# Linear attention, a gated mixer and a gated convolution: every engine's order from a list schedule, and the last weights split early through HBM

## The chip, the cores and the metric

The kernel runs on one core of a Trainium2 chip. The metric is the device time of one execution in microseconds.

## The reference, cut to what matters

All tensors are fp32, with B = 8 batches, H = 8 heads, S = 576 tokens, D = 64, d_model = 512 and d_ff = 1024. Three stages follow each other:

```python
# 1 attention: softmax of q over D, of k over S
kv = einsum('bhsd,bhse->bhde', softmax_s(k), v)
x  = einsum('bhsd,bhde->bhse', softmax_d(q), kv)      # to [B, S, 512]
# 2 gated mixer
h = gelu(x @ w_in); u, v = halves(h)
v_n = (v - mean) / sqrt(var + 1e-6) * g_ln
x = x + (u * (w_sg @ v_n + b_sg)) @ w_out
# 3 gated convolution over tokens
h = relu(x @ w_in2)                                   # [B, S, 1024]
out = (h * sigmoid(conv3(h, conv_w))) @ w_out2
```

## The kernel before, in words

Every large product is made of three single-pass matmuls (`mm3`, lines 62 to 65): each operand is split into a high part and a low part, and hi·hi, hi·lo and lo·hi are summed in PSUM. So each operand needs two vector steps: ScalarE copies the high part (a rounding copy), and VectorE or GpSimd subtracts it to get the low part. The weights arrive in a 64-bit format and are taken apart by `Split` (lines 70 to 151): a job loads a slice (line 92), and then ScalarE (lines 99, 102, 109), VectorE (lines 100, 101, 107, 110) and GpSimd (lines 111, 119, 120) make its high and low parts. There are 12 jobs of 512 columns for stage two's weights, one for the convolution's, and 32 jobs of 256 columns for stage three's: 16 for `w_in2` and 16 for `w_out2`, with four VectorE operations each, on the tiles `s` and `t`.

For each batch, stages one and two run these groups on TensorE: `back_kv` (line 349, 40 small products for k times v; `kvd` is the normalised result), `xt` and `xt_left` (lines 389 and 376: x from q and `kvd`, evacuated into `xh` and `xl`), `hv` (line 408, four token tiles and in five batches a fifth one, `hv_pair`, each of 12 matmuls of 512 columns), `hu` (line 458, 8 groups of 12 of 288 columns), `mx` (line 468, 8 groups of 14 of 288) and `wo` (line 489, 8 groups of 12 of 288). After an `hv` come gelu on ScalarE, the statistics and the normalisation on VectorE (`bn_stats`, lines 418 to 422), a power on GpSimd (line 421), and the split of the result into `vnh` and `vnl`. After an `mx` come `u` (line 479), `gh` and `gl` (lines 483 and 484). `x` before and after the mixer goes to HBM (`xld`, `x2d`). The softmaxes of the next batches' k and q are cut into steps (`k_steps`, `q_steps`, lines 215 and 274). Batch 0 has a softmax of its own, on other layouts (`s_k` to `s_qtl`, lines 560 to 608).

Stage three runs after all batches of stage two: `h2` (line 818, 16 groups of 12 matmuls of 288 columns for each batch), the convolution and the sigmoid (lines 830 to 841), and `o2` (line 857, 8 groups of 12 of 512 columns, with 24 more for each two batches for the left-over tokens).

What sets the order: a string (`CFG['start']`, line 32) gives the start, and `PLAN` says after which of the 29 groups of a batch a step of k, of q or of a weight split is put in. GpSimd keeps the order in which the code was written. The other engines' instructions are ordered by the framework's scheduler, which can also interleave the matmuls of different groups. The 32 jobs of stage three's weights run from batch 6's eighth group to the middle of stage three's first batch (`w2["in"].step()` and `w2["out"].step()`), since their buffers take the place of the attention's tiles.

Of the kernel before, what the change touches and what calls it, by code (L numbers as in the profile page):

```python
# [1 line left out]

# [19 lines left out]
PLAN = {  # L22
# [6 lines left out]
}  # L29
PLAN = {s: {i: [(c, 1) for c in t] for i, t in p.items()} for s, p in PLAN.items()}  # L30
# [4 lines left out]

@with_exitstack
def attn_gated_conv_kernel(ctx, tc, q, k, v, q0, k0, w_in, g_ln, w_sgT, b_sg, w_out, w_in2, conv_w, w_out2, out):
    nc = tc.nc
    dve, act, pool, pe, sp = nc.vector, nc.scalar, nc.gpsimd, nc.tensor, nc.sync
# [3 lines left out]
    ctx.enter_context(tc.manual_schedule(engines={mybir.EngineType.Pool}))  # L43
    dram = ctx.enter_context(tc.tile_pool(name="dram", bufs=1, space=bass.MemoryType.DRAM))
    ps_mm = ctx.enter_context(tc.tile_pool(name="ps_mm", bufs=4, space=bass.MemoryType.PSUM))
    ps_acc = ctx.enter_context(tc.tile_pool(name="ps_acc", bufs=1, space=bass.MemoryType.PSUM))
    keep = ctx.enter_context(tc.tile_pool(name="keep", bufs=1))
    xp = ctx.enter_context(tc.tile_pool(name="xp", bufs=1))

    x2d = [dram.tile([128, KC, S], F32, name=f"x2d{b}") for b in range(B)]  # L50
    xld = [dram.tile([128, KC, S], F32, name=f"xld{b}") for b in range(B)]

    def mm_tile():
        return ps_mm.tile([128, 512], F32, tag="mm", name="mm")
# [15 lines left out]
    class Split:  # L70
        def __init__(self, slots, jobs, mode):
            self.slots, self.jobs, self.mode = slots, jobs, mode
            self.loaded = self.done = 0

        def views(self, i):
            src, hi, lo, n = self.jobs[i]
            raw, a = self.slots[i % len(self.slots)]
            raw = raw[:, 0:2 * n].bitcast(U32)
            a = a[:, 0:n]
            if len(src.shape) == 4:  # L80
                g = src.shape[1]
                raw = raw.rearrange("p (g f two) -> p g f two", g=g, two=2)
                a = a.rearrange("p (g f) -> p g f", g=g)
                return src, raw, raw[:, :, :, 1], raw[:, :, :, 0], a, hi, lo
            raw = raw.rearrange("p (f two) -> p f two", two=2)
            return src, raw, raw[:, :, 1], raw[:, :, 0], a, hi, lo

        def load(self):
            i = self.loaded
            if i < len(self.jobs) and i < max(0, self.done - 1) + len(self.slots):  # L90
                src, raw = self.views(i)[0:2]
                sp.dma_start(raw, src)
                self.loaded += 1

        def p1(self, i):
            while self.loaded <= i:
                self.load()
            src, raw, h, l, a, hi, lo = self.views(i)
            act.activation(l.bitcast(F32), l, AF.Copy, scale=2.0 ** -52)
            dve.tensor_scalar(a.bitcast(U32), h, 3, 0x3FFFFFF8, ALU.logical_shift_left, ALU.bitwise_and)  # L100
            dve.scalar_tensor_tensor(a.bitcast(U32), h, 0xC0000000, a.bitcast(U32), ALU.bitwise_and, ALU.bitwise_or)  # L101
            act.activation(h.bitcast(F32), h.bitcast(F32), AF.Square)

        def p2(self, i):
            src, raw, h, l, a, hi, lo = self.views(i)
            lf, hf = l.bitcast(F32), h.bitcast(F32)
            dve.scalar_tensor_tensor(a, hf, GUARD * GUARD, a, ALU.is_ge, ALU.mult)
            if hi is not None:
                act.activation(hi, a, AF.Copy)  # L109
            dve.tensor_scalar(h, a.bitcast(U32), 0xFF800000, None, ALU.bitwise_and)  # L110
            (pool if hi is not None else dve).tensor_tensor(lf, lf, hf, ALU.mult)

        def p3(self, i):
            src, raw, h, l, a, hi, lo = self.views(i)
            if hi is None:
                dve.tensor_tensor(lo, a, l.bitcast(F32), ALU.add)
                return
            e1, e2 = self.mode(i)
            e1.tensor_tensor(a, a, r32(hi), ALU.subtract)
            e2.tensor_tensor(lo, a, l.bitcast(F32), ALU.add)  # L120

        def step(self):
            i = self.done
            if i > len(self.jobs):
                return
            if i > 0:
                self.p2(i - 1)
            if i < len(self.jobs):
                self.p1(i)
            if i > 0:  # L130
                self.p3(i - 1)
            self.done += 1
            self.load()

        def need(self, i):
            while self.done < i + 2:
                self.step()
# [22 lines left out]
    p1 = es1.enter_context(tc.tile_pool(name="p1", bufs=1, reuse_waits="tile"))  # L160
    wk = es1.enter_context(tc.tile_pool(name="wk", bufs=2, reuse_waits="tile"))
# [17 lines left out]
    at = es2.enter_context(tc.tile_pool(name="at", bufs=1, side="right", reuse_waits="tile"))  # L179
# [4 lines left out]
    scr = at.tile([128, 1024], F32, name="scr")  # L184
# [132 lines left out]
    class Stream:  # L317
# [657 lines left out]
```

## Time and profile before

| | |
|---|---|
| median of 3 runs | 1004.29 us (1003.51 to 1005.01) |
| the profiled execution | 1007.08 us, with a span of 1005.3 us |
| TensorE busy | 931.5 us (93%), 6080 matmuls |
| VectorE, ScalarE, GpSimd busy | 753.6, 450.8, 399.2 us |
| mean granted TensorE clock | 0.974 |
| DMA | 90.61 MB, 90 GB/s on average |

Busy time is the time in which an instruction of the engine was under way. Matmuls overlap in their pipeline, so what one costs is the distance from its start to the next one's start, not its duration. An engine works through its instructions in their order: one that waits holds up all behind it.

### The profile page before, as it was taken

The page shows a single profiled execution, that of the slowest core. Times are in us where ns is not written, and L with a number is a line of the kernel's source. Part 1 is how long each engine was busy: PE and PEld are TensorE (multiplying, and loading weights), DVE is VectorE, ACT ScalarE, POOL GpSimd, SP SyncE. Part 2 cuts the span into 40 slices and gives each one's busy share as a digit, 9 for nine tenths or more (in the row PEclk, how much of TensorE's full clock was granted, in tenths as well). Part 3 has the DMA queues.
Part 4 walks back from the last instruction along what each step waited for, and adds up shares of the span by engine and source line. Part 5 has one row for each costly group of instructions (what it writes and reads, how often), then busy time and mean ns, then how long its engine had stood idle before and what let it go on. Part 6 is the DMA issues. An engine that isn't in the chain of part 4 may idle for free.

```text
span 1005.3 us, 15903 instructions
## 1 busy us (share of the span) xinstructions
PE 931.5 (93%) x6080; PEld 835.1 (83%) x6080; DVE 753.6 (75%) x1354; ACT 450.8 (45%) x897; POOL 399.2 (40%) x469
## 2 busy tenths in 40 slices
PE   4665998989999999999989998899999999999998
PEld 3454977978989999898978987698999899989996
DVE  7999796867775676754888499787687758775863
ACT  6543635355536263361645355344344434443442
POOL 6447536437233071441575166632222322232210
PEclk9777998999999999999999999999999999999999
DMA  9721160451244212310332251213030303030001
GB/s 286 237 75 54 54 184 27 140 170 32 83 134 154 73 33 87 113 71 25 121 119 77 71 202 32 75 63 136 11 124 13 137 11 121 16 137 11 25 19 52
DMA packets 36580, 90.61 MB, mean 90 GB/s; under 512 B 3732, under 2 KB 14996, under 8 KB 32920
## 3 DMA queue, kind: packets, MB, share of 16 engines
q1 hardware_dynamic: 36504, 89.60, 27.4%
q8 instruction: 47, 0.77, 0.3%
q14 instruction: 29, 0.24, 0.1%
HBM read 62.46 MB, written 27.13 MB: 89 GB/s over the span
## 4 chain that ended last, share of the span: by engine, by line
PE 55%; DVE 22%; POOL 7%; issue 7%; ACT 6%; DMA 3%; SPq 0%; POOLq 0%; ACTq 0%; DVEq 0%
PE mm L63 10%; PE mm L65 10%; PE mm L64 10%; PE acc L63 7%; PE acc L64 7%; PE acc L65 7%; POOL kt L240 2%; POOL q L290 1%; DVE t L101 1%; PE mm L358 1%; DVE qm L285 1%; DVE t L100 1%; POOL rd L421 1%; DVE vnl L431 1%; DVE st L418 1%
## 5 line engine op out<-in xcount | busy, mean ns | idle before, releaser
L64 PE MATMUL mm<-xl,w2h 128*128 128x288 f32 x512 | 150.2, 295 | 0.6 <-DVE xl L813 0.6
L65 PE MATMUL mm<-xh,w2l 128*128 128x288 f32 x512 | 150.0, 295 | 0.0
L63 PE MATMUL mm<-xh,w2h 128*128 128x288 f32 x512 | 148.0, 295 | 1.9 <-ACT xh L812 1.9
L421 POOL TENSOR_TENSOR rd<-rd,nhalf 128x1 f32<-128x1 f32 x37 | 36.2, 982 | 176.2 <-DVE rd L420 171.0
L65 PE MATMUL acc<-wAh,yl 128*128 128x512 f32 x256 | 98.6, 393 | 4.7 <-DVE yl L841 4.7
L63 PE MATMUL acc<-wAh,yh 128*128 128x512 f32 x256 | 100.6, 393 | 1.6 <-ACT yh L840 1.6
L64 PE MATMUL acc<-wAl,yh 128*128 128x512 f32 x256 | 100.8, 394 | 0.0
L63 PEld LDWEIGHTS mm<-xh,w2h 128*128 128x128 f32 x512 | 95.2, 188 | 6.0 <-ACT xh L812 3.2
L64 PEld LDWEIGHTS mm<-xl,w2h 128*128 128x128 f32 x512 | 95.9, 188 | 3.8 <-DVE xl L813 1.4
L65 PEld LDWEIGHTS mm<-xh,w2l 128*128 128x128 f32 x512 | 96.0, 188 | 0.4
L65 PE MATMUL mm<-sgh,vnl 128*128 128x288 f32 x256 | 79.0, 309 | 8.2 <-DVE vnl L431 8.2
L65 PE MATMUL mm<-xh,wAl 128*128 128x288 f32 x256 | 77.2, 302 | 9.9 <-POOL wAl L120 6.3
L63 PE MATMUL mm<-sgh,vnh 128*128 128x288 f32 x256 | 81.7, 319 | 4.0 <-ACT v L414 2.2
L831 DVE SCALAR_TENSOR_TENSOR cv<-h,cw,cv 128x576 f32<-128x576 f32 x64 | 81.4, 1272 | 1.8
L63 PE MATMUL mm<-xh,wAh 128*128 128x288 f32 x256 | 79.4, 310 | 2.8 <-ACT wAh L109 2.7
L841 DVE TENSOR_TENSOR yl<-cv,yh 128x576 fp32r<-128x576 f32 x64 | 51.5, 804 | 37.5 <-ACT yh L840 37.4
L64 PE MATMUL mm<-sgl,vnh 128*128 128x288 f32 x256 | 78.3, 306 | 0.0
L64 PE MATMUL acc<-gl,wouth 128*128 128x288 f32 x256 | 74.1, 302 | 3.7 <-DVE gl L484 3.5
L838 ACT ACTIVATE cv<-cv 128x576 f32<-128x576 f32 x64 | 43.8, 686 | 74.5 <-DVE cv L832 73.9
L64 PE MATMUL mm<-xl,wAh 128*128 128x288 f32 x256 | 76.8, 300 | 0.0
L828 ACT ACTIVATE h<-mm 128x288 f32<-128x288 f32 x128 | 51.0, 407 | 54.6 <-PE mm L65 54.5
L844 POOL CAST yL1h<-yh 128x64 fp32r<-128x64 f32 x32 | 19.5, 611 | 139.3 <-ACT yh L840 139.3
(232 smaller groups left out, 2648.5 us busy)
## 6 DMA issues: line engine op xcount, KB each, us to landing
vt<-in_v SPq DMA_DIRECT2D x8, 1152.0 KB, 10.9
x2d<-x2s SPq DMA_DIRECT2D x16, 576.0 KB, 3.5
out<-ot SPq DMA_DIRECT2D x32, 256.0 KB, 2.0
kt<-in_k SPq DMA_DIRECT2D x7, 1152.0 KB, 5.3
xld<-xl SPq DMA_DIRECT2D x7, 1152.0 KB, 4.2
xf<-x2d SPq DMA_DIRECT2D x7, 1152.0 KB, 6.3
xg<-xld SPq DMA_DIRECT2D x7, 1152.0 KB, 5.1
q<-in_q SPq DMA_DIRECT2D x28, 256.0 KB, 2.9
```

Of the source, the lines that this page charges most:

```text
L63: pe.matmul(ps, ah, bh, start=start, stop=False)
L64: pe.matmul(ps, ah, bl, start=False, stop=False)
L65: pe.matmul(ps, al, bh, start=False, stop=stop)
L100: dve.tensor_scalar(a.bitcast(U32), h, 3, 0x3FFFFFF8, ALU.logical_shift_left, ALU.bitwise_and)
L101: dve.scalar_tensor_tensor(a.bitcast(U32), h, 0xC0000000, a.bitcast(U32), ALU.bitwise_and, ALU.bitwise_or)
L240: pool.tensor_tensor(kc, kc, bc, ALU.subtract)
L421: pool.tensor_tensor(rd, rd, nhalf, ALU.pow)
L828: act.activation(h[:, 1 + hf * HALF:1 + hf * HALF + HALF], ps, AF.Relu)
L831: dve.scalar_tensor_tensor(cv, h[:, 0:S], cw[:, fc:fc + 1], cv, ALU.mult, ALU.add)
L838: act.activation(cv, cv, AF.Sigmoid)
L841: dve.tensor_tensor(yl, cv, r32(yh), ALU.subtract)
L844: pool.tensor_copy(yL_hi[:, fc, o:o + 64], r32(yh[:, 512:576]))
```

## The change

Nothing that is computed changes, and the matmuls are the same. Three things change.

First, the kernel no longer issues instructions as its code runs. `Plan` records every instruction of all five engines, with the tile regions that it reads and writes (`View`, `Buf`, `Pool`), prices it with a formula per engine and operation (`price`), gives it a latest time that counts back from TensorE's groups in the order in which they were written (`deadlines`), and then runs a list schedule (`order`): at each moment a free engine takes the ready instruction with the earliest latest time. TensorE takes whole groups, the first of the next eight that would stall for at most 0.15 (the first) or 0.05. What comes out is issued in that order, and the framework orders nothing (`manual_schedule(engines=None)`). A formula for VectorE beside GpSimd lengthens both.

Second, `PLAN`, `Stream` and the string for the start are gone: `insert` says after which groups the attention of the next batch (`xt`, `back_kv`) and the softmax steps of the one after it (`attend_k`, `attend_q`) are recorded, and the schedule places them.

Third, the 32 split jobs are recorded at the start of batch 1 (`split_far`), work on two small slots (`wsl`, `farh`), and store their two halves to HBM (`w2d`, `wo2d`). After batch 6's attention is done, `open_w2` loads both halves back into SBUF, 8 loads of 128x4x256; `open_wo2` loads 16 of 128x512 late in batch 7. That adds 64 stores of 128x256 and 24 loads to SP's queue. The scratch tile of the k maxima is halved (`scr`), so `top` takes three maxima of 512 columns in place of one of 1024 and one of 512, and `h_t` of stage three moves to the pool of `w2`.

The core of the diff:

```diff
-    ctx.enter_context(tc.manual_schedule(engines={mybir.EngineType.Pool}))
+    plan = Plan({"pe": nc.tensor, "act": nc.scalar, "dve": nc.vector, "pool": nc.gpsimd, "sp": nc.sync})
+    dve, act, pool, pe, sp = plan.dve, plan.act, plan.pool, plan.pe, plan.sp
+    ctx.enter_context(tc.manual_schedule(engines=None))
...
-PLAN = {
-    0: {0: 'w', 1: 'ws', 2: 'sw', 3: 'ssw', 5: 'k', 8: 'wsw', 9: 'c', 11: 'qk', 12: 'ck', 14: 'w', 15: 'q', 16: 'kw', 18: 'kq', 19: 'kkq', 20: 'q', 21: 'q', 22: 'kqk', 23: 'qkqq', 25: 'qq', 27: 'kq', 28: 'qqw', 29: 'qqq'},
...
+    def deadlines(self):
+        t = 0.0
+        for n in self.nodes:
+            n.late = big
+            if n.eng == "pe":
+                n.late = t
+                t += n.cost
...
+        for n in reversed(self.nodes):
+            for s in n.succ:
+                c = n.lat if s.deps[n.i] == "end" else 0.0
+                n.late = min(n.late, s.late - c)
...
+            if n.eng == "dve" and n.shared and poolend[0] > t:
+                more = min(cost, poolend[0] - t) * 0.8
+                cost, lat = cost + more, lat + more
...
+    def split_far(src, d, k, n, behind):
+        for c in range(k):
+            for f in range(0, n, NW):
+                fs = slice(f, f + NW)
+                slot, h = parts[njob[0] % 2]
+                njob[0] += 1
+                split(slot, src[:, c, fs], far_h, slot[1].bitcast(F32R), NW, (pool, pool), [t[:, c, fs] for t in d], behind)
...
     def open_w2():
-        es2.close()
+        g = plan.gate(at.bufs, es2.close)
...
+            for n, d in zip(("hi", "lo"), w2d):
+                sp.dma_start(r32(w2[n][:, :, fs]), d[:, :, fs])
...
-            if (b == 6 and i >= 7) or (b == 7 and i < 24):
-                w2["in"].step()
-            if b == 7 and i >= 24:
-                w2["out"].step()
-                w2["out"].step()
+            if b == 1 and i == 0:
+                mark = next(n for n in reversed(plan.nodes) if n.eng == "pe")
+                split_far(w_in2_v, w2d, KC, FF2, mark)
+                split_far(w_out2_v, wo2d, NFC, DM, mark)
             g()
-            attend(b, i + 1)
+            insert(b, i)
```

How the instructions move, at the three places that the prediction speaks of, on VectorE and, at the third, on SP too. In the changed kernel all instructions are issued from one line, 394.

At the start, where batch 0's k times v is normalised into `kvd` (`rs` is the reciprocal of the sums; `wAl` and `sa` belong to a weight split, `qm` and `lm` to batch 1's softmax). Before:

```order
L365 TENSOR_SCALAR rs_278<-mm 128x2
L120 TENSOR_TENSOR wAl<-sb,sa 128x512
L107 SCALAR_TENSOR_TENSOR sa<-sa 128x24
L285 TENSOR_REDUCE qm<-q_351 128x16
L366 RECIPROCAL rs_278<-rs_278 128x2
L252 TENSOR_REDUCE lm<-q_255 128x8
L110 TENSOR_SCALAR sa<-sa 128x24
L285 TENSOR_REDUCE qm<-q_353 128x16
L369 TENSOR_TENSOR kvd<-mm,rs_278 64x2x64 x2
```

With the change:

```order
L394 TENSOR_TENSOR xl_0_122<-xl_0_122,wAh_238 128x512
L394 TENSOR_REDUCE sm_115<-sgh_91 128x4
L394 TENSOR_TENSOR sgh_91<-sgh_91,sm_115 128x256
L394 TENSOR_SCALAR rs_0_274<-mm_175 128x2
L394 RECIPROCAL rs_0_274<-rs_0_274 128x2
L394 TENSOR_TENSOR kvd_89<-mm_175,rs_0_274 64x2x64 x2
L394 TENSOR_REDUCE sm_115<-sgh_91 128x4
L394 TENSOR_SCALAR sm_115<-sm_115 128x4
```

The first `kvd` was VectorE's 51st row, with weight work and batch 1's softmax between its steps; now it is the 27th, with its steps together.

Near the end of batch 0, where batch 1's x is split into `xl` (the tile with number 1168 before, 948 now; `kt` and `scr` are the maxima of batch 2's k, `gl` the gate of batch 0). Before:

```order
L221 TENSOR_TENSOR scr<-scr 128x512
L384 TENSOR_TENSOR xLl<-mm,xLh 128x4x64
L395 TENSOR_TENSOR xl_1168<-mm,xh_1167 128x512
L484 TENSOR_TENSOR gl<-u,gh 128x288
L213 COPY qx<-qm 32x64 x4
L222 TENSOR_TENSOR scr<-scr,kt 64x256
L395 TENSOR_TENSOR xl_1168<-mm,xh_1167 128x512
L223 TENSOR_TENSOR scr<-scr,kt 64x256
```

With the change:

```order
L394 TENSOR_TENSOR scr_130<-scr_130,kt_149 64x256
L394 STREAM_TRANSPOSE scr_130<-scr_130 128x512
L394 TENSOR_TENSOR lt_0_324<-lt_0_324,wouth_745 128x512
L394 TENSOR_REDUCE r_0_494<-scr_130 128x16
L394 COPY r_0_519<-r_0_494 64x16 x2
L394 TENSOR_TENSOR r_0_494<-r_0_494,r_0_519 128x16
L394 COPY r_0_519<-r_0_494 32x16 x4
L394 TENSOR_TENSOR r_0_494<-r_0_494,r_0_519 128x16
L394 STREAM_TRANSPOSE scr_130<-r_0_494 128x512
L394 TENSOR_TENSOR xl_0_948<-mm_133,xh_0_902 128x512
```

Batch 1's `xl` stood behind nearly all of batch 0's gates, with batch 2's maxima between its parts. Now batch 2's maxima stand whole ahead of it, and half of batch 0's gates behind it: five of the eight `gl` have a later row.

The split of stage three's weights. Before, in batch 6, tiles `s` and `t`:

```order
L395 TENSOR_TENSOR xl_4883<-mm,xh_4882 128x512
L419 BN_AGGR mv<-st 128x2
L100 TENSOR_SCALAR t_4971<-s_4970 128x256
L420 TENSOR_SCALAR rd<-mv 128x1
L422 SCALAR_TENSOR_TENSOR v<-v,mv,g_bc 128x512
L101 SCALAR_TENSOR_TENSOR t_4971<-s_4970,t_4971 128x256
L100 TENSOR_SCALAR t_4973<-s_4972 128x256
L100 TENSOR_SCALAR t_4975<-s_4974 128x256
```

With the change, in batch 1, tile `wsl`:

```order
L394 TENSOR_SCALAR wsl_1266<-wsl_1266 128x256
L394 SCALAR_TENSOR_TENSOR wsl_1266<-wsl_1266 128x256
L394 TENSOR_TENSOR gl_848<-u_635,gh_826 128x288
L394 TENSOR_TENSOR xl_0_320<-mm_133,xh_0_306 128x512
L394 TENSOR_TENSOR xl_0_320<-mm_175,xh_0_306 128x512
L394 TENSOR_TENSOR u_681<-mm_187,u_681 128x288
L394 TENSOR_TENSOR gl_791<-u_681,gh_722 128x288
L394 TENSOR_TENSOR qm_373<-qm_373,qx_389 128x64
L394 TENSOR_TENSOR lm_369<-lm_369,lx_375 128x8
L394 SCALAR_TENSOR_TENSOR wsl_1266<-wsl_1266 128x256
```

The 128 VectorE operations of these jobs stood from batch 6 to stage three; now 12 stand in batch 1, 20, 20, 22, 30 and 24 in batches 2 to 6, one or two at a time, and none later. On SP the stores stand among the loads of the next batches, with the change (`q` is batch 5's, `x2d` takes batch 1's x after the mixer):

```order
L394 DMA w2dl_1683<-wsl_1266 128x256
L394 DMA x2d_0_1710<-x2s_124 512x1x288
L394 DMA w2dh_1611<-farh_1605 128x256
L394 DMA kt_149<-in_k 128x2304
L394 DMA vt_85<-in_v 128x36x64
L394 DMA wsl_1266<-in_w_in 128x512
L394 DMA w2dl_1683<-wsl_1266 128x256
L394 DMA q_1_135<-in_q 128x256
```

A store of a `farh` half stands right ahead of batch 4's k and v.

## Rows read from the trace of the kernel before

**Rows 1.** Busy time by stretch: length, PE, PEld, DVE, ACT, POOL, PE clock, DMA share, GB/s.

```profile
0.00:40.30 40.30, 18.79 (x132) 12.21 (x133) 34.66 (x73) 26.10 (x56) 22.97 (x32) 0.87 0.83 265
40.30:135.80 95.50, 73.37 (x456) 63.97 (x456) 86.16 (x145) 43.43 (x79) 54.88 (x46) 0.86 0.35 101
135.80:213.60 77.80, 71.27 (x542) 64.06 (x541) 58.65 (x144) 34.66 (x66) 38.76 (x39) 0.93 0.31 99
213.60:280.20 66.60, 64.35 (x469) 58.24 (x468) 50.56 (x115) 34.47 (x70) 26.12 (x26) 1.00 0.31 97
280.20:339.30 59.10, 59.10 (x446) 53.98 (x444) 38.92 (x97) 27.07 (x53) 16.66 (x17) 1.00 0.44 129
339.30:403.60 64.30, 63.42 (x465) 57.71 (x464) 45.19 (x97) 29.18 (x63) 26.23 (x26) 1.00 0.20 68
403.60:465.20 61.60, 60.76 (x449) 55.02 (x448) 37.39 (x86) 25.93 (x48) 20.70 (x21) 1.00 0.21 66
465.20:524.20 59.00, 57.07 (x358) 51.04 (x356) 46.45 (x100) 29.93 (x70) 33.49 (x42) 1.00 0.32 106
524.20:581.40 57.20, 53.44 (x353) 50.53 (x352) 37.54 (x85) 24.50 (x57) 22.53 (x29) 0.97 0.27 81
581.40:650.00 68.60, 59.24 (x352) 50.98 (x352) 62.54 (x103) 32.66 (x72) 46.83 (x56) 1.00 0.26 89
650.00:1005.30 355.30, 350.70 (x2075) 317.41 (x2073) 255.52 (x319) 142.87 (x267) 90.04 (x136) 1.00 0.18 65
```

**Rows 2.** Longest PE waits, whole span: us in total, times, longest.

```profile
PE mm L393 <- DVE kvd L369: 8.8, 1, 8.8
PE mm L65 <- DVE vnl L431: 8.2, 1, 8.2
```

**Rows 3.** Busy time, 75 to 100 us, columns as in Rows 1.

```profile
75.00:100.00 25.00, 12.96 (x60) 11.72 (x60) 22.98 (x20) 8.55 (x16) 19.49 (x16) 0.70 0.18 54
```

**Rows 4.** Timeline of DVE and then POOL near 84 us: start, duration, instruction.

```profile
83.88 8.97 DVE L670 TENSOR_TENSOR rhs<-sgs 2x576 fp32r<-2x576 f32 x1
...
87.32 4.91 POOL L240 TENSOR_TENSOR kt<-kt,scr 128x512 f32<-128x512 f32 x4
```

**Rows 5.** Timeline of PE: start us, duration, instruction; spacing of matmuls.

```profile
21.01 0.69 PE L358 MATMUL mm<-vt,kt 128*64 128x65 f32 x16
21.89 0.69 PE L358 MATMUL mm<-vt,kt 128*64 128x65 f32 x16
...
46.94 0.40 PE L63 MATMUL mm<-wAh,xh 128*128 128x512 f32 x1
51.63 0.39 PE L65 MATMUL mm<-wAh,xl 128*128 128x512 f32 x1
51.86 0.29 PE L63 MATMUL mm<-xh,wAh 128*128 128x288 f32 x1
53.56 0.29 PE L65 MATMUL mm<-xh,wAl 128*128 128x288 f32 x1
...
298.06 1.02 PE L393 MATMUL mm<-q,kvd 128*128 128x512 f32 x2
298.51 0.70 PE L63 MATMUL mm<-xh,wAh 128*128 128x288 f32 x1
...
1000.30 0.40 PE L65 MATMUL mm<-wAh,yL1l 128*128 128x512 f32 x1
```

**Rows 6.** Busy time on tile t, by stretch: length, DVE, ACT, POOL; the rest as Rows 1.

```profile
465.20:524.20 59.00, 23.70 (x50) 4.89 (x12) 19.33 (x24) 1.00 0.32 106
524.20:581.40 57.20, 16.39 (x35) 3.52 (x9) 13.44 (x17) 0.97 0.27 81
581.40:650.00 68.60, 22.47 (x45) 4.51 (x11) 22.93 (x24) 1.00 0.26 89
```

**Rows 7.** Line 100 on tile t: duration ns min/median/max, first and last start.

```profile
L100 DVE TENSOR_SCALAR t<-s x32: 262/316/873, 485.8 to 625.2; 128x256 uint32<-128x256 uint32 x32
```

**Rows 8.** Groups of ACT: one group of table loads.

```profile
L465 ACT ACT_TABLE_LOAD x9 | 11.5, 1283 | 1.6 <-DVE gl L484 1.4
```

More of the change, by code (lines that the diff above doesn't have):

```diff
@@ L68, in u64 @@
         return ap.bitcast(U32)
[L70 to L84, printed above, removed]
-            raw = raw.rearrange("p (f two) -> p f two", two=2)
[L86 to L137, printed above, removed]
@@ new lines, in split @@
+    def split(slot, src, hi, lo, n, modes, stores=(), behind=None):
+        raw, a = slot
+        raw = raw[:, 0:2 * n].bitcast(U32)
+        a = a[:, 0:n]
+        if len(src.shape) == 4:
+            g = src.shape[1]
+            raw = raw.rearrange("p (g f two) -> p g f two", g=g, two=2)
+            a = a.rearrange("p (g f) -> p g f", g=g)
+            h, l = raw[:, :, :, 1], raw[:, :, :, 0]
+        else:
+            raw = raw.rearrange("p (f two) -> p f two", two=2)
+            h, l = raw[:, :, 1], raw[:, :, 0]
+        lf, hf = l.bitcast(F32), h.bitcast(F32)
+        ld = sp.dma_start(raw, src)
+        if behind is not None:
+            ld.deps[behind.i] = "start"
+        act.activation(lf, l, AF.Copy, scale=2.0 ** -52)
+        dve.tensor_scalar(a.bitcast(U32), h, 3, 0x3FFFFFF8, ALU.logical_shift_left, ALU.bitwise_and)
+        dve.scalar_tensor_tensor(a.bitcast(U32), h, 0xC0000000, a.bitcast(U32), ALU.bitwise_and, ALU.bitwise_or)
+        act.activation(hf, hf, AF.Square)
+        dve.scalar_tensor_tensor(a, hf, GUARD * GUARD, a, ALU.is_ge, ALU.mult)
+        if hi is not None:
+            act.activation(hi, a, AF.Copy)
+        dve.tensor_scalar(h, a.bitcast(U32), 0xFF800000, None, ALU.bitwise_and)
+        (pool if hi is not None else dve).tensor_tensor(lf, lf, hf, ALU.mult)
+        if hi is None:
+            dve.tensor_tensor(lo, a, lf, ALU.add)
+            return
+        modes[0].tensor_tensor(a, a, r32(hi), ALU.subtract)
+        modes[1].tensor_tensor(lo, a, lf, ALU.add)
+        for t, d in zip((hi, lo), stores):
+            sp.dma_start(d, r32(t))
@@ L389, in xt @@
     def xt(b, hp):
+        plan.begin()
         if hp == 0:
@@ L408, in hv @@
     def hv(lh, ll, dst):
-        w1.need(3)
+        plan.begin()
         ps = mm_tile()
@@ L637, in s_sg @@
         sg_load(1)
[L639 to L651 removed]
+    for hp in range(4):
+        s_k(hp)
+    for t in range(5):
+        s_qa(t)
+    for hp in range(4):
+        s_kt(hp)
+    s_ktl()
+    for t in range(5):
+        s_qb(t)
+    for hp in range(4):
+        s_qt(hp)
+    s_qtl()
+    load_q(1)
+    load_left(1)
+    s_xl()
+    for c in range(2):
+        back_kv(0, c)
+    for hp in range(4):
+        xt(0, hp)
+    xt_left(0)
+    xt_copy(0)
+    for i, jb in enumerate(jobs):
+        split(slots[i % 3], *jb, MODES[i])
+        if i == 7:
+            split(csl[0], conv_v, None, cw, 3 * NFC, None)
+    s_sg()
     def sg_split(c):
@@ L759, in do_mx, with attend_k, attend_q, insert @@
         mx(b, j)
-    cj = Split(csl, [(conv_v, None, cw, 3 * NFC)], None)
-    cj.load()
+    def attend_k(b):
+        for f in k_steps(b):
+            f()
+    def attend_q(b):
+        for f in q_steps(b):
+            f()
+    def insert(b, i):
+        if b + 1 < B:
+            if b == 0 and i == 4:
+                attend_k(1)
+                attend_q(1)
+            if b == 0 and i in (8, 9):
+                back_kv(1, i - 8)
+            if b == 0 and i == 10:
+                xt_left(1)
+            if i in ((12, 14, 16, 18) if b % 2 == 0 else (8, 10, 12, 14)):
+                xt(b + 1, (i - (12 if b % 2 == 0 else 8)) // 2)
+            if b + 2 < B:
+                if i == 19:
+                    attend_k(b + 2)
+                    attend_q(b + 2)
+                if i in (23, 24):
+                    back_kv(b + 2, i - 23)
+                if i == 25:
+                    xt_left(b + 2)
+        if b == 6 and i == 20:
+            open_w2()
+        if b == 7 and i == 24:
+            open_wo2()
+        if b == 7 and i in (20, 21, 22, 23, 24):
+            x2_early(i - 20)()
     for b in range(B):
         if b == 1:
-            lt1[1] = p1.tile([128, DM], F32R, tag="lt11", name="lt11")
+            lt1[1] = p1.tile([128, DM], F32R, tag="lt11")
         groups = [lambda t=t: do_hv(b, t) for t in range(4)]
         groups += [lambda j=j: do_hu(b, j) for j in range(2)]
-        groups.insert(CFG['hvl'][min(b, 2)], lambda: do_pair(b))
+        groups.append(lambda: do_pair(b))
         for j in range(8):
```

553 lines of the change are left out of this document (401 added, 152 removed), and 5 rows, old and new, of the table PLAN.

## The prediction

> **What bounds the kernel now.** I read the busy time by stretch first, cut at the first `hv` matmul of each batch and at stage three's first `h2` (581.4 us) [rows 1]. The reader is to see three regimes. Until 135.8 us VectorE is the fullest engine (34.66 of 40.3 us, 86.16 of 95.5) while TensorE works 73.37 of 95.5, at a granted clock of 0.86, a mix of its two levels. Batches 2 to 7 (213.6 to 581.4) keep TensorE at 93 to 100%, with VectorE at 61 to 79%. From 581.4 to 650 VectorE is up to 62.54 of 68.6 and TensorE idles; after 650 TensorE is the bound. Then the longest waits of TensorE [rows 2]: 8.8 us for the first `kvd`, 8.2 us for a `vnl`, both on VectorE. In the stretch around the second, TensorE was busy 12.96 of 25 us and VectorE 22.98 [rows 3]. There one VectorE subtraction took 8.97 us, while GpSimd ran four subtractions of `kt` of 4.91 us [rows 4].
>
> **What TensorE must do.** The spacing of matmuls [rows 5] gives: 20 steps of 512 columns in 4.69 us, 0.2345 each; 13 steps of 288 in 1.70 us, 0.131 each; ten `kv` products in 0.88 us, 3.5 for 40; an `xt` pair 0.46, four of them 1.84; 0.8 for the left-over x is my estimate from that. A batch has 48 x 0.2345 = 11.3, 304 x 0.131 = 39.8, and 3.5 + 1.8 + 0.8: 57.2 us, or 60.0 with an `hv_pair` (2.8). Batches 2 to 7 need 60.0, 57.2, 60.0, 57.2, 55.7 (no `kv` left) and 51.1 (no attention left): 341.2. Stage three needs 1536 x 0.131 + 864 x 0.2345 = 403.8.
>
> **The change, part by part.** I cut the span in three.
>
> *A, to batch 2's first `hv`: 213.6 us now.* VectorE works 34.66 + 86.16 + 58.65 = 179.5 of it and idles 5.6, 9.3 and 19.2 [rows 1]. The new order moves work in: 12 split operations at 62.56 / 128 = 0.49 us [rows 6], 5.9 us, and softmax work of later batches that now stands ahead of x (the second place), about as much again, 5.7 us, by my estimate from the rows moved. That makes 191. It also takes waits out: the first `kvd` is VectorE's 27th row and no longer its 51st (the first place), and five of batch 0's `gl` stand behind batch 1's `xl`. Of the idle time I keep the 5.6 (first loads), about half of 9.3 (4.4) and a third of 19.2 (7), since the schedule puts a ready instruction where VectorE used to wait: 191 + 17 = **208**. The lower end is 189: idle 6, and 8 of the 8.97 us subtraction gone as well. The upper end is 225: all 34 us stay. I take a value between the ends because the first two stretches are work, not waiting.
>
> *B, batches 2 to 7 without the last 3.1 us of `wo`, which run after 581.4: 367.8 + 3.1 = 370.9 now.* Above its need each batch lost 6.6, 1.9, 4.3, 4.4, 3.3 and 9.2 us. The edits with one price are the moved jobs. VectorE: batches 2 to 6 work 218.5 us, of which 23.70 were splits [rows 1, 6]; the other 194.8 and 116 operations of 0.49 make 251.5 of the 290.1 us that TensorE needs, 87%. GpSimd: tile `t` alone cost 55.70 [rows 6]; with the third operation of a job, taken as alike, some 82 for 96, which brings it to some 61%. ScalarE gets 41 table loads for 25, 16 x 1.283 = 20.5 us [rows 8], on an engine busy half the time. So each engine has room on average, and what is lost is order: 3.1 us a batch, between the best batch now (1.9) and the usual one (4.4): 341.2 + 18.6 = **359.8**. Ends: 352.6 (1.9 each) and 389 (the third rival).
>
> *C, stage three: 423.9 - 3.1 = 420.8 now*, which is 403.8 + 5.0 from the last matmul to the end [rows 5] + 12.0 lost. The 22.47 us of splits in 581.4 to 650 [rows 6] are gone, and with them the reason why TensorE idled 9.4 us there [rows 1]. I leave 2 us: 403.8 + 5.0 + 2 = **410.8**; ends 409 and 421 (if the loss is the convolution's own).
>
> Costed at nothing: the 64 stores of 128 KB and 24 loads (8.4 MB each way), since the DMAs move 66 to 129 GB/s in the batches and 265 in the first stretch [rows 1], and the queue of SP has one sequence of work. What stands behind a store that waits there is the next but one batch's k and v (the third place), two batches before use. If that cover fails, the time of one job on VectorE, 62.56 / 32 = 2 us, comes on top in a batch. The reload of `w_in2` is covered by batch 7; if it is late, `h2` waits for one load, about 3 us by my estimate from the stretch at 265 GB/s (two loads of 0.5 MB, 4 us, less what is under way). The extra maximum of `top` is one VectorE operation in a softmax on 512 columns, inside the 87%.
>
> Sum: 208 + 359.8 + 410.8 = 978.6 against a span of 1005.3. The profiled execution is 1007.08, 1.8 over its span, and the median of the runs 1004.29, 2.8 under that: 978.6 + 1.8 - 2.8 = 977.6, **978 us**.
>
> **The rivals.** *First, the start gives more.* If VectorE's idle time falls to the first loads' and the subtraction beside GpSimd takes its usual time, A is 189 and the total 959. For it: VectorE is the bound there, and the change orders it throughout. Against: the schedule fixes order, not work, and 19.2 us of the idle time may be a chain through GpSimd and ScalarE.
>
> *Second, the gain at the end is given back.* If the start does not shorten (213.6) and batches 2 to 6 each lose what batch 2 loses now, 6.6, with 3.1 in batch 7, B is 377.3; with C at 410.8 the total is 1001.7 - 1.0 = 1001. For it: the order rests on fixed durations, and a late engine holds all behind it. Against: 4 of 6 batches now lose under 4.5 with steps strewn between the groups.
>
> *Third, slower: VectorE becomes the bound in batches 2 to 6 through GpSimd.* The 96 GpSimd operations of the splits move beside batches whose VectorE work is 87% full. Line 100 takes 316 ns in the median and 873 at most on the same shape [rows 7], and the subtraction took 8.97 us beside GpSimd's [rows 4]: a VectorE operation can wait for the end of a GpSimd one. The free time is 290.1 - 251.5 = 38.6 us; above 0.4 us of hold-up for each of the 96, VectorE decides. The row with both engines so loaded is 581.4 to 650: TensorE busy 59.24 of 68.6, 13.6% idle. That share on 341.2 is 46: B 387.2, A 216 (the start too), C 410.8: 1014 - 1 = 1013. Against: that stretch holds two jobs' steps in a row, and the change spaces them.
>
> The Trainium skill's page "SBUF — State Buffer", section "Who interferes with whom", speaks for the third rival: a VectorE instruction with two SBUF inputs contends with a GpSimd instruction that reads SBUF, and of such a lock it says "Whoever issues first gets the shared pair for the whole instruction". By it alone, GpSimd's 82 us of splits could fall wholly on VectorE, and the free 38.6 us would be overdrawn by 43. The 8.97 us row agrees with it; the median of 316 ns says that most operations of line 100 did not pay.
>
> **How the numbers follow.** The forecast has 0.53: its three parts rest on rows that repeat. The first rival has 0.20, the second 0.10, the third 0.17. The range goes from 950 (the first rival with 1.9 us lost per batch, 951, and a little for its spacings) to 1013 (the third rival's figure); beyond both ends lies some 0.15. 0.2%, 2 us, is about what a measurement of this kernel can tell from no change. Forecast, first rival and most of the second lie below that: faster 0.77; same 0.05, between the second and third; slower 0.18.
>
> **What would show it.** Right: batch 2's first `hv` near 208 us; batches 2 to 7 within 3 us of 60.0, 57.2 and so on; VectorE at 80 to 90% in batches 2 to 6; stage three's first batch without idle TensorE. Wrong: a wait of TensorE for `gl`, `u` or `vnl` in each batch (third rival); VectorE operations that come out at twice their median in batches 2 to 6; k's or q's loads that land after VectorE wants them, behind a store; an `h2` that waits for a reload; TensorE's clock at the lower level after 213.6 us.

## The result and the profile after

The changed kernel is slower by 1.1%: 1015.74 us (median of 4, 1012.38 to 1016.01) against 1003.9 (median of 4, 1002.6 to 1005.01), a ratio of 1.0111 with an interval of 1.0086 to 1.0135. The profiled execution is its fastest, 1012.38 with a span of 1010.6, so the two traces differ by 5.3 us where the medians differ by 11.8.

Busy time by stretch of the changed kernel, cut as [rows 1] at the first `hv` of batches 0 to 7 and at the first `h2` (columns as there):

```profile
0.00:31.94 31.94, 19.22 (x133) 12.67 (x133) 23.51 (x48) 18.43 (x35) 16.23 (x28) 0.95 0.95 294
31.94:159.86 127.92, 82.54 (x551) 70.88 (x551) 121.08 (x224) 62.34 (x118) 78.45 (x66) 0.79 0.37 113
159.86:223.31 63.45, 61.71 (x450) 55.57 (x449) 54.85 (x119) 40.96 (x75) 33.49 (x37) 1.00 0.34 107
223.31:291.71 68.40, 65.09 (x462) 58.05 (x461) 58.83 (x127) 44.85 (x90) 39.32 (x42) 0.98 0.39 121
291.71:357.03 65.32, 62.30 (x462) 56.27 (x461) 56.72 (x124) 38.22 (x76) 37.09 (x41) 1.00 0.46 139
357.03:425.14 68.11, 63.62 (x450) 57.67 (x449) 51.84 (x113) 38.54 (x78) 32.31 (x36) 0.95 0.39 124
425.14:488.48 63.34, 62.07 (x463) 56.36 (x462) 48.21 (x110) 28.69 (x57) 28.96 (x36) 1.00 0.37 114
488.48:548.77 60.29, 58.46 (x374) 53.21 (x373) 35.59 (x86) 24.76 (x54) 20.75 (x27) 1.00 0.50 166
548.77:600.50 51.73, 51.73 (x354) 49.44 (x353) 23.47 (x52) 14.07 (x29) 3.94 (x4) 1.00 0.40 131
600.50:1010.60 410.10, 405.47 (x2402) 365.99 (x2400) 284.09 (x366) 160.81 (x305) 96.05 (x156) 1.00 0.19 66
```

Part A takes 223.3 us (before 213.6, forecast 208), part B 377.2 (370.9, forecast 359.8), part C 410.1 (420.8, forecast 410.8). The end came as forecast: batch 7 takes 51.73 us with TensorE never idle, and the loss of [rows 1] between 581.4 and 650 is gone. The start did not: from 31.94 to 159.86 VectorE is busy 121.08 of 127.92 us and TensorE's granted clock is 0.79 on average. By batch 1's first `hv` VectorE has worked 144.6 us, 24 more than before (120.8). In batches 2 to 6 TensorE idles up to 4.5 us in each although VectorE is busy only 77% of the time (251.19 of 325.46).

Cuts at an `hv` don't hold equal work, since the schedule regroups TensorE's work. So I counted both kernels' 6080 matmuls in order of their start, each at the spacing that it has where TensorE does not wait, and read when each kernel has done the same work. The spacings are 0.1325 us (288 columns), 0.2343 (512), 0.0466 (k times v), 0.434 (x, two records for each `xt`), 0.111 (left-over x) and 0.214 (transposes). The lag of the changed kernel behind the one before, in us:

```
work done  before is at   changed kernel's lag
   70 us       127 us           +19.0
  100          158              +18.5
  160          230               +9.5
  220          293              +12.4
  270          343              +16.4
  310          383              +23.5
  440          519              +22.1
  500          587              +15.0
  560          659               +3.0
  900          996               +5.2
```

It loses 18.5 us in the first 100 us of work, wins half of it back by 230 us, loses 14 between 160 and 310 us of work, and wins 19 between 440 and 560, where the splits of stage three's weights used to be. The last 2 us grow evenly through stage three, and no run here explains them. (The lags in the expectations below come from a coarser count and are mostly some 1 to 3 us lower.) Of the longest waits of TensorE (total, times, longest), these are now the ones that differ; the 8.8 us for `kvd` of [rows 2] has shrunk to 0.9, and the 8.2 for `vnl` to 0.3:

```profile
PE mm L394 <- ACT wAh L394: 17.9, 2, 11.3
PE mm L394 <- DVE xl L394: 9.8, 2, 8.6
...
PE mm L394 <- DVE wAl L394: 6.9, 2, 4.2
PE mm L394 <- DVE lt L394: 6.1, 2, 4.2
...
PE mm L394 <- POOL wAl L394: 4.8, 1, 4.8
```

Before, the waits for the same tiles `wAh` and `wAl`, stage two's weights, were:

```profile
PE mm L65 <- POOL wAl L120: 6.3, 2, 3.6
...
PE mm L65 <- DVE wAl L120: 3.6, 1, 3.6
...
PE mm L63 <- ACT wAh L109: 2.7, 1, 2.7
```

So TensorE waits 29.6 us for these weights at the start where it waited 12.6, 17 us more and the largest rise of any wait there. TensorE's clock adds to it: of the first 100 us of work, 16.2 ran at the lower of its two granted levels (0.5), at half the pace, and 12.3 before. The 8.60 us for `xl` stand on VectorE and then TensorE near 130 us: batch 2's maxima (`scr`, `r`; their last step is shown) run first, then batch 1's `xl`, and TensorE starts again behind it:

```profile
129.34 0.71 DVE L394 STREAM_TRANSPOSE scr<-r 128x512 f32<-128x512 f32 x1
129.98 1.25 DVE L394 TENSOR_TENSOR xl<-mm,xh 128x512 fp32r<-128x512 f32 x2
...
130.69 0.61 PE L394 MATMUL mm<-sgh,vnh 128*128 128x288 f32 x1 [8.60 <-DVE xl L394]
```

The wait for `lt` is 4.17 us at its longest, in batch 4, seen on GpSimd, VectorE, ScalarE and TensorE:

```profile
371.47 4.85 POOL L394 TENSOR_TENSOR kt<-kt,scr 128x512 f32<-128x512 f32 x3
376.28 0.67 POOL L394 TENSOR_TENSOR rd<-rd,nhalf 128x1 f32<-128x1 f32 x1
...
375.08 1.26 DVE L394 TENSOR_TENSOR lm<-lm,lx 128x8 f32<-128x8 f32 x1
...
378.87 1.28 ACT L394 ACT_TABLE_LOAD   x1
380.17 2.12 ACT L394 ACTIVATE kt<-kt 128x2304 f32<-128x2304 f32 x1
382.20 1.32 ACT L394 ACTIVATE lt<-v,rd 64x512 fp32r<-64x512 f32 x2
...
383.87 0.61 PE L394 MATMUL mm<-rhs,lt 128*128 128x288 f32 x1 [4.17 <-DVE lt L394]
```

GpSimd does three subtractions of `kt` in 4.85 us before it gives the power for `rd`; beside them a maximum of 128x8 takes VectorE 1.26 us; and ScalarE loads a table and takes the exponential of all of `kt` (1.28 + 2.12 us) before it makes the `lt` that TensorE wants. Each engine works through its list, and the lists no longer fit each other. From 381.7 to 388.5 us TensorE's granted clock is 0.50, so this wait costs more than its own length.

### The profile page after: what moved, and what is told of

Its sections match the earlier page's. It is cut to its first block, busy times and chain, and to the rows that moved or that the text cites. A ratio compares the mean times of both kernels' runs of the same rounds, so it can differ in the third digit from the quotient of the medians.

```text
span 1010.6 us, 16155 instructions
## 1 busy us (share of the span) xinstructions
PE 932.2 (92%) x6080; PEld 836.1 (83%) x6080; DVE 758.2 (75%) x1361; ACT 471.7 (47%) x913; POOL 386.6 (38%) x469
## 5 line engine op out<-in xcount | busy, mean ns | idle before, releaser
L394 PE MATMUL mm<-xh,w2h 128*128 128x288 f32 x512 | 151.3, 295 | 0.0
L394 DVE SCALAR_TENSOR_TENSOR cv<-h,cw,cv 128x576 f32<-128x576 f32 x128 | 117.5, 918 | 4.0
L394 PE MATMUL acc<-wAh,yl 128*128 128x512 f32 x256 | 101.5, 396 | 0.0
L394 PE MATMUL acc<-gh,wouth 128*128 128x288 f32 x256 | 80.9, 316 | 0.3 <-ACT gh L394 0.3
L394 DVE TENSOR_TENSOR cv<-cv,h 128x576 f32<-128x576 f32 x64 | 51.8, 809 | 38.0 <-ACT cv L394 37.9
L394 PE MATMUL acc<-gh,woutl 128*128 128x288 f32 x256 | 76.6, 299 | 3.6 <-DVE woutl L394 3.6
L394 PE MATMUL acc<-gl,wouth 128*128 128x288 f32 x256 | 77.3, 302 | 2.8 <-DVE gl L394 2.7
L394 POOL TENSOR_TENSOR q<-q,qm 128x512 f32<-128x512 f32 x56 | 63.0, 1151 | 37.1 <-DVE qm L394 30.9
```

The costliest lines, as they stand in the source:

```text
L394: getattr(self.real[n.eng], n.name)(*[val(a) for a in n.args], **{k: val(v) for k, v in n.kw.items()})
```

## The experiments

Two theories at first. **Prices**: the plan's durations for VectorE beside GpSimd are too short, so its lists put steps ahead that are late on the chip. Added up by the kernel's own formulas (`price`, `order`), the plan charges VectorE 697.8 us where the trace has 758.2, and ends at 968.5 us where the trace ends at 1010.6; it also knows no lower clock of TensorE. **Load**: the far splits' work on VectorE and GpSimd is what batches 2 to 5 lost. A third, **places**, says that where the softmax steps are recorded decides. The lags behind the kernel before, read as above (first column the changed kernel):

```
work  changed   e1     e2     e5     e7     e8     e9    e10
  70   +19.0  +20.3  +15.4  +15.5   +8.9  +18.7   +5.7  +16.0
 100   +18.5  +19.8  +17.0  +17.1  +13.2  +18.2  +14.7  +20.4
 160    +9.5  +11.0   +7.5   +7.4   +4.8  +10.1   +4.4  +11.2
 220   +12.4  +10.4   +8.4   +6.7   +6.0  +15.4   +3.1  +12.4
 310   +23.5  +15.1  +10.5  +11.9  +14.2  +26.4  +10.0  +17.0
 440   +22.1   +9.6   +6.8   +6.4  +14.2  +27.3   +5.4  +13.2
 560    +3.0   -9.5  -12.2  -12.8   -4.9   +8.1  -13.6   -5.8
```

**e1, the far splits' work on VectorE and GpSimd left out, and half of ScalarE's.** In `split_far`, per job:

```diff
-                split(slot, src[:, c, fs], far_h, ...)
+                ld = sp.dma_start(raw, src[:, c, fs])
+                act.activation(slot[1], raw[:, :, 0], AF.Copy, scale=2.0 ** -52)
+                act.activation(far_h, raw[:, :, 1], AF.Copy, scale=2.0 ** -52)
+                for o, e in zip((r32(far_h), slot[1]), d):
+                    sp.dma_start(e[:, c, fs], o)
```

> This kernel is the changed one with VectorE's and GpSimd's work on the 32 far split jobs left out (the loads, two of the four ScalarE copies, the 64 stores and the 24 reloads stay; the two halves that it stores are not the weights' halves). The changed kernel spends 64.6 us of VectorE and 70.9 us of GpSimd on them in batches 1 to 6. Theory F (that load is what batches 2 to 5 lost, 13 us against the kernel before): the median falls from 1015.7 to about 1002, and the lag behind the kernel before no longer grows after 230 us. Theory O (the loss comes from the order, which waits wherever the plan's durations were too short): it falls by under 5 us, and the lag of 16 us at 170 us stays in both.

Measured: 998.86 us, 0.9942 of before (0.9926 to 0.9957), 17 us under the changed kernel. The work of the jobs can be seen in the sum of the changed kernel's stretches on the tile `wsl`, 159.86 to 548.77 us, and what is left out in the busy times of e1's page:

```profile
sum 388.91, DVE 64.62 ACT 39.77 POOL 70.89; mean DVE 10.77 ACT 6.63 POOL 11.82
```

```profile
PE 928.9 (93%) x6080; PEld 836.0 (84%) x6080; DVE 698.3 (70%) x1233; ACT 459.8 (46%) x881; POOL 314.6 (32%) x373
```

The lag of the start stays (19.8 at 100 us of work), and from 160 to 310 the lag grows by 4 and no longer by 14. Theory load fits so far, but so does prices, since this work is also what the plan misjudges. The same work costs the 32 jobs' VectorE steps 64.62 us here and 62.56 in [rows 6]: it did not become dearer by being moved.

**e2, the price of a held-up operation.**

```diff
             if n.eng == "dve" and n.shared and poolend[0] > t:
-                more = min(cost, poolend[0] - t) * 0.8
+                more = poolend[0] - t
```

> One line of the planner changes: a VectorE operation that shares with GpSimd is priced as held up until the GpSimd operation under way ends, and no longer by 0.8 of the shorter of the two. Theory P (the plan's short prices beside GpSimd make it put softmax steps ahead of what TensorE waits for): at least half of the 16 us lost in the first 170 us and of the 13 lost in batches 2 to 5 come back, median about 1000. Rival S (the places where the softmax steps are recorded decide, since the latest times are fixed by them): within 5 us of 1015.7.

Measured: 997.96 us, 0.9929 of before (0.9905 to 0.9953), 17.8 us under the changed kernel, with all its work kept. Theory prices holds, against load: VectorE still does all 64 of these operations, over a longer stretch (last start 569.4 us; 526.9 in the changed kernel):

```profile
L394 DVE TENSOR_SCALAR wsl<-wsl x64: 229/295/1131, 196.0 to 569.4; 128x256 uint32<-128x256 uint32 x64
```

In the stretch of the `lt` wait, 370 to 386 us, TensorE was busy 11.51 of 16 us in the changed kernel and is busy 15.36 in e2, whose work there is some 13 us further on (length, PE, PEld, DVE, ACT, POOL, clock, DMA, GB/s):

```profile
370.00:386.00 16.00, 11.51 (x70) 10.55 (x69) 13.38 (x25) 12.01 (x21) 11.83 (x12) 0.87 0.06 19
```

```profile
370.00:386.00 16.00, 15.36 (x105) 13.93 (x104) 12.09 (x25) 13.56 (x21) 9.38 (x10) 1.00 0.14 42
```

At equal work, from 160 to 310 us, the lag grows by 3 in e2 and by 14 in the changed kernel. With this line the plan charges VectorE 744.0 us and the trace has 753.9, so most of the 60 us that were missing are in it.

But the expectation was wrong for the start: at 100 us of work the lag is 17.0, hardly less than the 18.5 without the edit. Here batch 2's maxima do run behind most of batch 1's `xl` (130.1 us after 125.1) and the wait for `xl` is gone, but TensorE still waits 24.2 us for stage two's weights.

**e5, both edits.**

> Both edits at once: the planner's price of the full hold, and the far splits' work left out as in the run that kept their loads, two ScalarE copies and stores (the stored halves are not the weights'). If the two edits gave back the same us (the price helps because it takes the far splits' hold-ups of VectorE into account), the median is 990 to 998, under 8 us below the kernel with the price alone (998). If they are independent, the gains add: 998 - 17 = 981.

Measured: 996.13 us (0.9909, 0.9876 to 0.9942), 1.8 under e2, with overlapping intervals. So the two gains are one: under the price of the full hold, the far splits' work on VectorE and GpSimd costs batches 1 to 6 next to nothing, and without that work the short price costs only 2.7 (e1 against e5).

**e10, a longer price for all of VectorE.**

```diff
+            if n.eng == "dve":
+                cost, lat = cost * 1.066, lat + cost * 0.066
             if n.eng == "dve" and n.shared and poolend[0] > t:
```

> The planner keeps its 0.8 rule beside GpSimd, and each VectorE operation is planned 6.6% longer, which adds as much planned VectorE time in all as the price of the full hold did. Theory P (it matters which operations are held, and when): 1008 to 1016. Rival U (any plan that gives VectorE as much time as it really takes is good enough): within 4 us of the 998 of the full hold.

Measured: 1003.92 us, 0.9999 of before (0.9989 to 1.0009), below what theory prices expected and above what its rival did. So 11.8 of the 17.8 us come back by giving VectorE more time in all. That the other 6 come from giving it to the operations that are held is not shown, since the two runs do not add the same: the plan charges VectorE 737.7 us here and 744.0 in e2. Nor did a run lengthen the prices of another engine, or VectorE's by another amount, so how much any disturbance of the list gains is not told; e3 and e8 below disturb it too and gain nothing.

**e8, less GpSimd, more VectorE.** `(pool, pool)` becomes `(dve, dve)` in the jobs' call of `split`.

> The two subtractions and additions of each far job go from GpSimd to VectorE: GpSimd is spared 64 operations of about 0.74 us (47 us), VectorE gets 64 of about 0.42 (27 us). If what costs is GpSimd's operations holding VectorE and its own short operations (the power of the normalisation, the subtractions of k): the lag gained in batches 2 to 5 halves, 1006 to 1012. If what costs is VectorE's load: it grows, 1018 to 1030.

Measured: 1018.42 us, 1.0136 of before (1.0101 to 1.0172), 2.7 above the changed kernel with overlapping intervals. The median lies at the lower edge of what theory load expected. With 46.6 us less on GpSimd (340.0) and 27.4 more on VectorE (785.6) the lag in batches 2 to 5 is larger by 3 to 5 us. So what GpSimd is spared does not make up for what VectorE gets under the same short prices.

**e6, the list schedule without the way through HBM.** `split_far` is called where the weights are opened, and its jobs write straight into the tiles.

> The list schedule alone: the 32 split jobs are recorded where the weights are opened, at the end of batches 6 and 7, and write straight into their tiles; no halves go through HBM. If the far splits cost batches 2 to 5 what the run without them showed (12 us by 300 us, 17 in all) and bring 20 us at the end: the lag behind the kernel before stays at 9 to 14 us through batches 2 to 5, and the end keeps the kernel before's loss of 15 to 20 us or more, median 1018 to 1030. If the place of the splits does not matter: 1010 to 1017.

Measured: 1058.88 us, 1.0535 of before (1.0505 to 1.0565), worse than either theory said. Through batches 2 to 5 its lag grew by little (18.0 at 180 us of work, 20.3 at 310, 14.8 at 440), as expected without the splits; then TensorE waits once for 48.80 us, with the jobs of `w_out2` ahead of the first `yh` on ScalarE:

```profile
661.18 0.79 PE L394 MATMUL acc<-wAh,yh 128*128 128x512 f32 x1 [48.80 <-ACT yh L394]
```

These jobs have only two slots and wait for their loads in turn, so the 48.8 us is a price of this form too; the plan itself already ends 55 us later (1023.6 us). The early split with its way through HBM is 43 us better than this late one; how much a good late split would lose (the kernel before: 19 us of lag) is not told by this run.

**e3, batch 2's softmax later.** In `insert`:

```diff
-                if i == 19:
+                if i == 19 and b > 0:
                     attend_k(b + 2)
                     attend_q(b + 2)
-                if i in (23, 24):
+                if i in (23, 24) and b > 0:
                     back_kv(b + 2, i - 23)
...
+            if b == 1 and i == 0:
+                attend_k(2)
+                attend_q(2)
+            if b == 1 and i in (4, 5):
+                back_kv(2, i - 4)
```

> Batch 2's softmax is recorded after batch 1's first group and no longer after batch 0's 20th, its k times v after batch 1's groups 5 and 6. Theory S (batch 2's maxima stand on VectorE ahead of batch 1's x, and TensorE waits 8.6 us for it at 122 us): that wait goes and the median falls by 8 to 14 us, to 1002 to 1008. Theory P: VectorE has as much to do before and TensorE waits elsewhere, within 4 us of 1015.7.

Measured: 1016.61 us, 1.0117 of before (1.0081 to 1.0153), no different. Batch 2's maxima still run just ahead of `xl`, and TensorE still waits 7.74 us:

```profile
126.64 2.64 DVE L394 TENSOR_TENSOR scr<-scr,kt 128x512 f32<-128x512 f32 x3
129.31 1.29 DVE L394 TENSOR_TENSOR xl<-mm,xh 128x512 fp32r<-128x512 f32 x2
...
130.05 0.61 PE L394 MATMUL mm<-sgh,vnh 128*128 128x288 f32 x1 [7.74 <-DVE xl L394]
```

The edit moved where the steps are recorded and hardly where they run, since their latest times stayed. So it does not test whether they cost something ahead of `xl`; e2, where they run behind `xl` and the start is hardly faster, says that they cost little.

**e7, batch 1's softmax later.** Batch 1's k times v and x follow it (groups 14, 15 and 18 to 24), and batch 2's steps move to groups 25 to 28:

```diff
-            if b == 0 and i == 4:
+            if b == 0 and i == 9:
                 attend_k(1)
                 attend_q(1)
-            if b == 0 and i in (8, 9):
-                back_kv(1, i - 8)
+            if b == 0 and i in (14, 15):
+                back_kv(1, i - 14)
...
-                if i == 19:
+                if i == (25 if b == 0 else 19):
```

> Batch 1's softmax and attention are recorded five to six groups later in batch 0, batch 2's six and three groups later. Theory S1 (batch 1's softmax runs on VectorE and GpSimd beside the stage-two weights, which took 60.2 us of VectorE for 48.8 before, and TensorE waits for the weights): the lag at 150 us falls from 16 to under 8 us, median 1003 to 1009. Rival (the weights' own chain, three slots and their loads, sets the start): the lag at 80 us stays over 10, median within 5 us of 1015.7.

Measured: 1005.3 us, 1.0003 of before (0.9989 to 1.0017), 10.4 under the changed kernel. The lag at 70 us of work falls from 19.0 to 8.9, but at 100 us of work (158 us in the kernel before) it is 13.2 for 18.5, so the expected fall to under 8 us at 150 us did not come; at 80 us of work it is 13.2 as well, over the 10 that the rival named, though the median is the one of theory S1. From 160 to 310 it still grows by 9. What TensorE waits for at the start is still weights, 27.7 us for 29.6, but the wait for `xl` has gone from the longest ones:

```profile
PE mm L394 <- ACT wAh L394: 12.5, 2, 6.5
...
PE mm L394 <- POOL wAl L394: 8.3, 3, 4.6
...
PE mm L394 <- DVE wAl L394: 6.9, 2, 4.2
PE acc L394 <- DVE gl L394: 6.8, 5, 3.9
```

So the early place of batch 1's (or batch 2's) attention cost the start some 5 of its 18.5 us, and the other 13 stay. The rival, that the weights' own chain of jobs sets the start, was not tested by a run that moves the weights, and it is open. One cost of the early place shows in the stage-two weights. Two groups of 8 VectorE operations of their split, up to 130 us, in the kernel before and in the changed one (total, mean ns):

```profile
L100 DVE TENSOR_SCALAR sb<-sa 128x512 uint32<-128x512 uint32 x8 | 3.8, 478 | 0.7 <-DMA sa<-in_w_out 0.7
L101 DVE SCALAR_TENSOR_TENSOR sb<-sa,sb 128x512 uint32<-128x512 uint32 x8 | 5.7, 707 | 0.1
```

```profile
L394 DVE TENSOR_SCALAR xl<-xh 128x512 uint32<-128x512 uint32 x8 | 8.9, 1117 | 0.0
L394 DVE SCALAR_TENSOR_TENSOR xl<-xh,xl 128x512 uint32<-128x512 uint32 x8 | 8.6, 1076 | 0.2
```

478 and 707 ns became 1117 and 1076, 8 us more for 16 operations. In e7 these two groups take 726 and 1116, so 3 of the 8 us came back and the rest did not. The plan of e7 itself ends 9.3 us before that of the changed kernel (959.2 for 968.5), so this gain is one that the plan saw, with its short prices.

**e4, TensorE's groups as written.**

```diff
-    WINDOW = 8
+    WINDOW = 1
```

> TensorE takes its groups in the order in which they are written (a window of one group for eight). Rival W (the regrouping of TensorE's work, which puts batch 1's k times v ahead of batch 0's later groups at 88 us, costs the start): faster than 1015.7 by 5 us or more. Theories S and P: the regrouping hides waits and without it the time is longer, 1016 to 1040.

Measured: 1034.59 us, 1.0303 of before (1.027 to 1.0337). The regrouping of TensorE's work hides waits and is worth 19 us; the rival W falls.

**e9, the price and the places.** The edits of e2 and e7.

> Both edits that helped: the price of the full hold and batch 1's (and 2's) softmax recorded later. They act at different places (the price in batches 2 to 6, the places in the first 150 us), so the gains should add: 998 less 6 to 10 is 988 to 992, faster than both kernels. If the price already moved what the places move: 995 to 999.

Measured: 996.15 us, 0.9908 of before (0.9894 to 0.9922), faster than both kernels by 8 to 9 and by 20 us; but only 1.8 under e2, with overlapping intervals. The lag at 70 us of work is 5.7 and not 15.4, yet at 100 us it is 14.7 for 17.0: most of what was won is lost again within 30 us of work. At 160 and 220 it is 3 and 5 better than e2, and at 310 the same. From 100 to 160 us VectorE is busy 54.80 of 60 us in e9, 55.61 in e2 and 55.54 in the changed kernel, so a wait that an order takes out there comes back elsewhere. Its stretches from 160 us on:

```profile
160.00:500.00 340.00, 333.74 (x2414) 302.88 (x2413) 284.46 (x619) 198.81 (x393) 171.36 (x188) 0.99 0.39 120
500.00:600.00 100.00, 100.00 (x690) 95.25 (x689) 59.98 (x134) 39.48 (x88) 27.75 (x37) 1.00 0.62 207
```

From 160 to 600 us TensorE is busy 433.74 of 440 us, which leaves little room for gains to add.

## Why the prediction was wrong

The forecast was 978 us, with a range of 950 to 1013. The time lies just above it, by the third rival's sum (1013), but not by its mechanism: its parts were A 216, B 387.2 and C 410.8, measured were 223.3, 377.2 and 410.1, so the sum is near by luck. Nearest in mechanism was the second rival (1001), that a late engine holds all behind it: its B was 377.3, but it left A as it was.

**Part C and batch 7 were right.** 410.1 us for 410.8, and batch 7 in 51.73 for a need of 51.1. Moving the splits away from 465 to 650 us brought what the rows said; no `h2` waited for a reload.

**VectorE's load in batches 2 to 6 was right.** It was forecast at 251.5 us there and did 251.19; that it agrees to 0.3 is luck, since the stretches no longer hold the same work. GpSimd did 158.4 us, where the forecast of 61% of 290.1 meant 177. The third rival needed VectorE to be full; it was at 77%. The sign of TensorE's lower clock came, for 10.2 us after batch 2's first `hv`, behind waits for `lt`.

**What fell in part B is the term of 3.1 us lost per batch**, "between the best batch now (1.9) and the usual one (4.4)". Two things were wrong in it. The need was too low: an `xt` was priced at 0.46 us, the distance to the next matmul. That distance is not the whole cost here. The rest of it falls on the distance behind the next one, as the changed kernel's trace shows too:

```profile
391.37 1.02 PE L394 MATMUL mm<-q,kvd 128*128 128x512 f32 x2
391.83 0.70 PE L394 MATMUL mm<-sgh,vnh 128*128 128x288 f32 x1
392.37 0.29 PE L394 MATMUL mm<-sgl,vnh 128*128 128x288 f32 x1
```

From 391.83 to 392.37 stands one matmul of 288 columns, 0.54 us where 0.13 is its own: some 0.87 us for an `xt`, the usual figure in both traces, and 1.6 us more for four. With 288 columns at 0.1325 us for 0.131, and k times v at 3.7 for 3.5, a batch with all its attention needed 2.4 us more than I counted, and part B 12 in all. So of the 20.5 us that batches 2 to 6 "lost" in [rows 1] some 12 were work, and nothing was to be won in them. Against that need they lost 1.8 us each before, not 4.1, and lose 4.7 with the change; batch 7 lost 8.8 and loses 0.2. That is the second mistake: the change made the loss per batch larger where I had it smaller. The room that an engine has on average says nothing when each engine's list is fixed by prices. The hold-ups between VectorE and GpSimd are not in the plan at their length (697.8 us planned for 758.2), e2 alone brings 17.8 us back, and e5 shows that the splits' load costs next to nothing once they are.

**In part A the step "the schedule puts a ready instruction where VectorE used to wait" failed.** VectorE did 199.4 us up to batch 2's `hv` where I had 191, and idled 24 where I had 17. It filled waits with batch 1's and 2's softmax, which stood ahead of what TensorE wanted, and operations of the weights' split became dearer (8 us for the 16 above). TensorE's waits for stage two's weights rose from 12.6 to 29.6 us, a term that the forecast put at nothing. The prediction had named the second place, batch 2's maxima whole ahead of `xl`, and read it as work moved in; it is the place of the 8.60 us wait, on an engine that was already full. But with that wait gone in e2 the start is hardly faster. e7 gives back some 5 of the 18.5 us, and it moves the softmax, the k times v and x of batch 1 and those steps of batch 2 together, so which of them carries its 10.4 us is not taken apart. Why the weights come later, which is most of the start's loss, stays open.

**The rule of the Trainium skill** ("SBUF — State Buffer", "Who interferes with whom") was weighed for the third rival, and its lock is there: the rows of the last section show it. By it alone GpSimd's split work would have fallen on VectorE; the measured sum of the splits' steps (64.62 us for 62.56 before) and VectorE's whole busy time (758.2 for 753.6) say that in sum VectorE's work became hardly dearer than it was.

## What to carry to other kernels

A static order is only as good as its prices: sum up, engine by engine, what the plan charges and what the trace shows, and price an operation that another engine can hold by the rest of that engine's operation, before the order itself is changed. When an edit is to move a step, look in the trace whether it moved: e3's did not. Room on average does not protect an engine whose list is fixed; look for what stands ahead of the one step that TensorE waits for next. And when a "loss" per stage is to be won back, check by the distances around each kind of instruction that it is not work.

## What the runs showed of the hardware

Which VectorE operations GpSimd holds up is sharply divided. Duration min/median/max in ns of operations of the changed kernel, whole span:

```profile
L394 DVE TENSOR_SCALAR wsl<-wsl x64: 229/295/1378, 186.5 to 526.9; 128x256 uint32<-128x256 uint32 x64
...
L394 DVE TENSOR_TENSOR gl<-u,gh x64: 395/458/1517, 103.7 to 598.4; 128x288 fp32r<-128x288 f32 x64
...
L394 DVE TENSOR_TENSOR lm<-lm,lx x7: 103/581/1256, 40.5 to 375.1; 128x8 f32<-128x8 f32 x7
...
L394 DVE TENSOR_TENSOR u<-mm,u x64: 411/457/459, 96.9 to 597.4; 128x288 f32<-128x288 f32 x64
...
L394 DVE BATCH_NORM_STATS2 st<-v x37: 646/686/696, 54.6 to 561.3; 128x6 f32<-128x512 f32 x37
...
L394 DVE TENSOR_REDUCE qm<-q x56: 629/675/687, 39.3 to 418.2; 128x16 f32<-128x512 f32 x56
```

Those with two SBUF inputs (`gl`, `lm`) and the 128x256 shift of the splits, which has one, reach nearly four to twelve times their shortest; the product with a PSUM input (`u`), the statistics and the reductions never vary by more than 12%, though they run beside GpSimd too. The same page and section of the Trainium skill say that an instruction with one SBUF input outside the two-port modes does not contend. The rows of `u`, `st` and `qm` agree; the shift is held, and no row here tells in which mode it runs. A held operation ends a good part of its own length after the GpSimd operation under way, as here at 67.7 and 69.4 us (GpSimd's ends: 67.4, and 68.9 for the first of its three of 1.51 us):

```profile
66.09 1.62 DVE L394 TENSOR_SCALAR xl<-xh 128x512 uint32<-128x512 uint32 x1
67.74 1.64 DVE L394 SCALAR_TENSOR_TENSOR xl<-xh,xl 128x512 uint32<-128x512 uint32 x1
...
65.58 1.84 POOL L394 TENSOR_TENSOR sgl<-x2s,sgh 128x576 fp32r<-128x576 f32 x1
67.38 4.53 POOL L394 TENSOR_TENSOR kt<-kt,scr 128x512 f32<-128x512 f32 x3
```

Even a 128x8 operation of 103 ns can take 1256; the planner leaves out everything up to 60 columns.
